# Linear attention: key-value product folded into the output weight, inverse denominators broadcast by DMA, against normalising each attention tile on its own

## The chip, the cores and the metric

The kernel runs on one core of a Trainium2 chip. The metric is device time in microseconds (us) of the whole program; several executions of each kernel are timed, and the median is quoted. The engines have short names in the profile: PE is TensorE (matmuls), PEld its weight loads, DVE is VectorE, ACT is ScalarE, POOL is GpSimd, SP is SyncE, which here only issues DMA transfers. Executions of one kernel agree within about one per cent.

## The reference, cut to what matters

```
def _A_ref(x, wqkv, wo):              # S = 2048 rows, D = 1024, H = 32 heads of 32
    qkv = (x @ wqkv)...               # q, k, v per head
    phi = lambda t: where(t > 0, t + 1, exp(t)) + 1e-6
    pq, pk = phi(q), phi(k)
    kv = einsum("bhsd,bhse->bhde", pk, v)       # 32 x 32 per head
    z = einsum("bhsd->bhd", pk)
    num = einsum("bhqd,bhde->bhqe", pq, kv)
    den = einsum("bhqd,bhd->bhq", pq, z)[..., None] + 1e-6
    return (num / den)... @ wo
x = A_x
h = x + _A_ref(layernorm(x), A_wqkv, A_wo)
h2 = h + _B_ref(layernorm(h), ...)    # a token-mixing MLP: most of the matmul work
```

Because the division is per row and head, `(pq @ kv / den) @ wo` equals `(pq / den) @ (kv @ wo)` when each head's 32 columns of `pq` are scaled first. `kv @ wo` has no row of the sequence in it, so it can be computed once.

## The kernel before

Queries come out transposed: `pqT[p, j, s]` holds feature `j*128+p` (four heads in each group j of 128) of row s. A "q unit" is one group j of 512 rows: eight matmuls, then exp, relu, minimum and a sum. Once the key-value product is complete, each tile i of 128 rows is treated on its own, among the q units of the next 512 rows:

```python
def attn_num_den(i):
    for j in range(ND):                               # ND = 8
        nc.tensor.matmul(nd_ps[:, b, sl*NCOL:(sl+1)*NCOL],   # NCOL = 128 + 4
            lhsT=pqT[:, j, i*P:(i+1)*P], rhs=ndrhs[:, j, :], start=True, stop=True)
    dn = ...; nc.scalar.activation(dn..., ACT.Ln, bias=eps_den[:], scale=1.0)
    rd = ...; nc.scalar.activation(rd[:], dn[:], ACT.Exp, scale=-1.0)     # 1/den
    for b in range(NNB):                              # three PSUM banks
        nc.vector.tensor_tensor(o_sb..., blk[:, :, 0:P]..., rd....to_broadcast(...), ALU.mult)
    return o_sb
def attn_transpose(i, o_sb):
    nc.sync.dma_start_transpose(out=pqT[:, :, i*P:(i+1)*P], in_=o_sb[:])
```

Then the output projection adds the residual. It runs tile by tile:

```python
def out_proj(i):
    xr = xrs.pop(i)                                   # a tile of x, loaded by SyncE
    for dc in range(NDC):                             # two halves of 512 columns
        ap_ = acc_tile()                              # ring of five PSUM banks
        nc.scalar.copy(ap_[:, 0:CW], xr[...])         # seeds the residual
        for j in range(ND):
            nc.tensor.matmul(ap_[:, 0:CW], lhsT=pqT[:, j, i*P:(i+1)*P], rhs=wo_sb[:, j, ...], ...)
        nc.scalar.copy(h_bf[...], ap_[:, 0:CW])
        nc.vector.bn_stats(st[:, dc, :], ap_[:, 0:CW])   # last reader: frees the bank
    ...
    nc.sync.dma_start(h_dram[i][:], h_bf[:])
```

A scheduler puts the instructions of every engine in an order at build time; `pin` keeps an instruction in the order of the program.

## Time and profile before

The median is 573.3 us (572.9 to 573.36, four runs).

| before | us |
|---|---|
| profiled span | 571.5 |
| PE busy | 563.7 (99%) |
| stretch from the first q unit after the key-value product to the mixer's first matmul | 104.4, PE busy in all of it |
| eight num/den matmuls of a tile | 0.47 |
| eight matmuls of 512 columns | 1.73 |

The busy table and the chain that ended last, from the page of the kernel before (share of the span by engine):

```profile
PE 563.7 (99%) x3124; PEld 293.3 (51%) x3124; DVE 390.2 (68%) x759; ACT 272.0 (48%) x585; POOL 1.8 (0%) x8
...
PE 95%; DVE 3%; ACT 1%; issue 1%; DMA 1%; ACTq 0%
```

The same kernel's busy time by windows; columns are the window, its length, and busy us of PE, PEld, DVE, ACT and POOL with counts of instructions, then the granted PE clock and the mean share of the 16 DMA engines and GB/s:

```profile
131.10:235.50 104.40, 104.40 (x577) 51.08 (x576) 81.36 (x196) 72.30 (x173) 0.00 (x0) 1.00 0.59 147
```

TensorE has no idle time there, so only slots on TensorE count. Slots are read as differences of starts, not as durations, since matmuls overlap: below, a group with a duration of 0.63 us holds back the next one by only 0.47. From the timeline of PE (start, duration, what):

```profile
138.47 0.63 PE L1118 MATMUL nd_ps<-ndrhs,pqT 128*128 128x132 bf16 x8
138.94 3.61 PE L1019 MATMUL acc_t<-xnT,wq_sb 128*128 128x512 bf16 x16
142.39 0.63 PE L1118 MATMUL nd_ps<-ndrhs,pqT 128*128 128x132 bf16 x8
...
235.50 1.68 PE L297 MATMUL psA<-hE,wq 128*128 128x512 f16 x7
237.34 0.38 PE L297 MATMUL psA<-hE,wq 128*128 128x512 f16 x1 [0.15 <-DVE hE L1189]
237.55 1.67 PE L297 MATMUL psE<-hE,sa 128*128 128x512 f16 x7
239.96 1.02 PE L297 MATMUL psA<-hO,wq 128*128 128x512 f16 x4 [0.74 <-ACT psB L316]
```

The eight num/den matmuls hold back the next group by 138.94 - 138.47 = 0.47 us; 16 tiles cost 7.5 us. The last rows are the step into the mixer, where PE waited for 0.15 and 0.74 us.

### The profile page before, as it was taken

Reading aid. Unit: us, or ns where it says so; the run is one execution under the profiler, and the core shown is the slowest. Engines: PE = TensorE matmul, PEld = TensorE weight load, DVE = VectorE, ACT = ScalarE, POOL = GpSimd, SP = SyncE. Lnnn points to the kernel's source line nnn. Section 1 sums busy time; section 2 is a strip of 40 time slices with the busy share of each in tenths; the row PEclk is TensorE's granted clock in tenths of the full one; section 3 lists DMA queues with packets and bytes.
Section 4 is the critical chain, followed back from the end, with each engine's and each line's share of the span. In section 5 each row is a group of like instructions: output and inputs, shape, how many; then the busy total and the mean of one; then the engine's idle time right before and its main releaser. Section 6 shows DMA issues by size and latency. Waiting matters only on the chain.

```text
span 571.5 us, 8308 instructions
## 1 busy us (share of the span) xinstructions
PE 563.7 (99%) x3124; PEld 293.3 (51%) x3124; DVE 390.2 (68%) x759; ACT 272.0 (48%) x585; POOL 1.8 (0%) x8
## 2 busy tenths in 40 slices
PE   7999999999999999999999999999999999999997
PEld 3444444455554444346555565555445655645643
DVE  6898887546767879873735627453979749659625
ACT  4747777666667776445445354453220411311211
POOL 1000000000000000000000000000000000000000
PEclk9999999999999999999999999999999999999999
DMA  9933432029536753104041340413892932912111
GB/s 303 357 76 79 89 74 38 19 96 323 118 72 127 177 178 111 55 2 147 1 148 28 120 148 1 148 48 81 205 255 84 244 96 75 278 56 73 38 47 46
DMA packets 97800, 66.61 MB, mean 117 GB/s; under 512 B 32082, under 2 KB 91744, under 8 KB 97760
## 3 DMA queue, kind: packets, MB, share of 16 engines
q1 hardware_dynamic: 97024, 65.42, 41.7%
q10 hardware_dynamic: 672, 0.66, 0.3%
q8 instruction: 24, 0.39, 0.3%
q14 instruction: 16, 0.13, 0.1%
q0 software_dynamic: 64, 0.01, 0.0%
HBM read 50.34 MB, written 8.39 MB: 103 GB/s over the span
## 4 chain that ended last, share of the span: by engine, by line
PE 95%; DVE 3%; ACT 1%; issue 1%; DMA 1%; ACTq 0%
PE psB L297 10%; PE psC L297 10%; PE acc_t L1019 9%; PE acc_t L1167 9%; PE psC L208 7%; PE psA L297 7%; PE psI L230 7%; PE psB L208 6%; PE psI L208 6%; PE psB L750 4%; PE psC L750 4%; PE psA L750 4%; PE psA L208 3%; PE acc_t L674 2%; PE psE L750 2%; PE psE L297 1%
## 5 line engine op out<-in xcount | busy, mean ns | idle before, releaser
L297 PEld LDWEIGHTS <-sa 128*128 128x128 f16 x436 | 42.6, 98 | 46.8 <-issue 0.7
L1019 PE MATMUL acc_t<-xnT,wq_sb 128*128 128x512 bf16 x256 | 58.0, 379 | 0.0
L1167 PE MATMUL acc_t<-wo_sb,pqT 128*128 128x512 bf16 x256 | 56.1, 379 | 0.0
L208 PEld LDWEIGHTS <-wq 128*128 128x128 bf16 (+1 forms) x357 | 34.5, 98 | 31.3
L297 PEld LDWEIGHTS <-wq 128*128 128x128 bf16 (+1 forms) x324 | 31.6, 98 | 33.1 <-issue 1.0
L208 PE MATMUL psC<-gs,wq 128*128 128x512 f16 (+2 forms) x210 | 45.0, 365 | 0.0
L1167 PEld LDWEIGHTS <-pqT 128*128 128x128 bf16 x256 | 24.8, 98 | 29.0
L1019 PEld LDWEIGHTS <-wq_sb 128*128 128x128 bf16 x256 | 24.5, 98 | 27.4
L166 ACT ACTIVATE e_sb<-acc_t 128x512 bf16<-128x512 f32 x40 | 23.9, 597 | 26.5 <-PE acc_t L1019 24.3
L170 DVE TENSOR_SCALAR e_sb<-e_sb 128x512 bf16<-128x512 bf16 x64 | 18.5, 289 | 25.4 <-ACT e_sb L166 24.8
L208 PEld LDWEIGHTS <-sa 128*128 128x128 f16 x231 | 22.6, 98 | 18.6
L750 PEld LDWEIGHTS <-xs 128*128 128x128 f16 x208 | 20.0, 98 | 23.3 <-DVE xs L736 1.3
L208 DVE TENSOR_TENSOR ot<-ot,hr 128x512 bf16<-128x512 bf16 (+2 forms) x27 | 11.2, 415 | 28.1 <-ACT ot L406 27.7
L333 ACT COPY psC<-psB 128x512 f32<-128x512 f32 x22 | 12.5, 570 | 35.1 <-PE psB L297 21.5
L297 PE MATMUL psB<-hT,sa 128*128 128x512 f16 x112 | 28.4, 379 | 0.0
L441 DVE TENSOR_TENSOR e<-psI,es 128x256 f32<-128x256 f32 x12 | 5.1, 425 | 34.0 <-PE psI L230 34.0
L297 PE MATMUL psC<-hT,wq 128*128 128x512 f16 x112 | 28.3, 379 | 0.0
L750 PE MATMUL psA<-wkv,xnT 128*128 128x512 bf16 x104 | 26.7, 379 | 0.0
L1178 DVE BATCH_NORM_STATS2 hst<-acc_t 128x6 f32<-128x512 f32 x32 | 22.1, 692 | 6.7 <-ACT h_bf L1177 6.5
L297 PE MATMUL psA<-hO,wq 128*128 128x512 f16 x112 | 25.6, 379 | 0.7 <-ACT psB L316 0.7
L297 PE MATMUL psB<-hO,sa 128*128 128x512 f16 x112 | 25.5, 379 | 0.0
L297 PE MATMUL psC<-hT,sa 128*128 128x512 f16 x112 | 25.5, 379 | 0.0
(184 smaller groups left out, 1022.9 us busy)
## 6 DMA issues: line engine op xcount, KB each, us to landing
wq<-in_B_w_dram SPq DMA_DIRECT2D x14, 1024.0 KB, 7.7
wq<-in_B_w_dram SPq DMA_DIRECT2D x8, 1792.0 KB, 9.1
xr<-in_A_x_dram SPq DMA_DIRECT2D x16, 256.0 KB, 3.1
h_dram<-h_bf SPq DMA_DIRECT2D x16, 256.0 KB, 2.2
hr<-h_dram SPq DMA_DIRECT2D x32, 128.0 KB, 2.4
out_dram<-ot SPq DMA_DIRECT2D x31, 128.0 KB, 1.8
x_sb<-in_A_x_dram SPq DMA_DIRECT2D x15, 256.0 KB, 3.2
wkv<-in_A_wqkv_dram SPq DMA_DIRECT2D x2, 1024.0 KB, 9.0
```

Source lines behind the costliest of these rows:

```text
L166: pin(nc.scalar.activation(e_sb[:], src, ACT.Exp))
L170: pin(nc.vector.tensor_scalar(e_sb[:], e_sb[:], 1.0, PHI_EPS, ALU.min, ALU.add))
L208: return (lambda *a, **kw: pin(op(*a, **kw))) if Held.on else op
L230: pe.matmul(ps, lhsT=self.lhs[m][:, k, :], rhs=self.mov[m][:, k, :], start=(start and k == 0), stop=(k == self.nk - 1), skip_group_check=True,
L297: pe.matmul(ps[:, cols], lhsT=lhs[:, k, :], rhs=mv(k)[:, cols], start=(start and k == 0), stop=(k == self.nk - 1), skip_group_check=True,)
L333: nc.scalar.copy(self.C[:], self.B[:])
L441: dve.tensor_tensor(self.sts[m].e[:, self.cols(h)], ps, es, ALU.add)
L674: mm = nc.tensor.matmul(pp[:, 0:CW], lhsT=xnT[:, kt, i * P:(i + 1) * P], rhs=wkv[:, kt, c * CW:(c + 1) * CW], start=(kt == 0), stop=(kt == ...
L750: pin(nc.tensor.matmul(ps[:], lhsT=lhs[:, k, :], rhs=rhs[:, k, :], start=(start and k == 0), stop=(k == hk2 - 1), skip_group_check=True,))
L1019: nc.tensor.matmul(qp[:, 0:SW], lhsT=wq_sb[:, kt, j * P:(j + 1) * P], rhs=xnT[:, kt, u * SW:(u + 1) * SW], start=(kt == 0), stop=(kt == ND ...
L1167: nc.tensor.matmul(ap_[:, 0:CW], lhsT=pqT[:, j, i * P:(i + 1) * P], rhs=wo_sb[:, j, dc * CW:(dc + 1) * CW], start=(j == 0 and not SEED_RES ...
L1178: nc.vector.bn_stats(st[:, dc, :], ap_[:, 0:CW])
```

## The change

The intent: replace 128 short matmuls, 48 VectorE evictions and 16 transposing DMAs by one multiplication of wo with the key-value product (8 transposes and 16 matmuls of 512 columns), by 32 matmuls for the denominators, and by scaling the transposed queries in place (8 products on VectorE). The denominators now come out transposed as well (one row per head), so a head's row must be spread over that head's 32 partitions; this is done through DRAM, with a source that repeats. The pieces, with cuts marked by dots:

```diff
-            def attn_transpose(i, o_sb):
-                nc.sync.dma_start_transpose(out=pqT[:, :, i * P:(i + 1) * P], in_=o_sb[:])
...
+            wf = wo_sb[:].bitcast(FP16)           # the folded weight is written over wo
+
+            def fold(j):
+                for c in range(NDC):
+                    cols = slice(c * CW, (c + 1) * CW)
+                    ps = acc_tile()
+                    nc.tensor.matmul(ps[:, 0:CW], lhsT=kvT[:, j, :], rhs=wo_sb[:, j, cols], start=True, stop=True)
+                    if c == 0:
+                        nc.scalar.copy(wf[:, j, cols], ps[:, 0:CW])
+                    else:
+                        nc.vector.tensor_copy(wf[:, j, cols], ps[:, 0:CW])
...
+            def den(u):                           # u: 512 rows
+                ps = ndp.tile([P, SW], F32, tag="den", name="den_ps")
+                for o in range(2):
+                    for g in range(4):            # four column tiles of the array
+                        j = 2 * g + o
+                        nc.tensor.matmul(
+                            ps[g * QR:(g + 1) * QR, :],                   # QR = 32
+                            lhsT=zz[:, j, (1 - o) * HB:(1 - o) * HB + QR],  # HB = 4 heads
+                            rhs=pqT[:, j, u * SW:(u + 1) * SW],
...
+                            tile_position=(0, g * QR),
+                        )
+                rd = a3d.tile([P, SW], FP16, tag="rd", name="rd")
+                nc.scalar.activation(ps[:], ps[:], ACT.Ln, bias=eps_den[:], scale=1.0 / S)
+                nc.scalar.activation(rd[:], ps[:], ACT.Exp, scale=-1.0)
+                pin(nc.sync.dma_start(rd_dram[u][:], rd[:]))
+                for h in range(2):
+                    rdb = a3d.tile([P, NH, SW], FP16, tag="rdb", bufs=3, name="rdb")
+                    for q in range(NH):           # four transfers of 128 KB
+                        j = h * NH + q
+                        r0 = (j // 2) * QR + (j % 2) * HB
+                        pin(nc.sync.dma_start(
+                            rdb[:, q, :],
+                            rd_dram[u][r0:r0 + HB, :].unsqueeze(1).to_broadcast([HB, DH, SW]),
+                        ))
+                    rdbs[u, h] = rdb
+                    if 0 < u < 3:
+                        load_w1(u - 1, h, pin)
+
+            def scale_q(u, h):
+                v = pqT[:, h * NH:(h + 1) * NH, u * SW:(u + 1) * SW]
+                pin(nc.vector.tensor_tensor(v, v, rdbs.pop((u, h))[:], ALU.mult))
...
             for i in range(NS):
-                if i % 2 == 0 and i // 2 < TPC:
-                    attn(NS - TPC + i // 2)
+                if i == 0:
+                    den(NSC - 1)
+                elif i in (1, 3):
+                    scale_q(NSC - 2, i // 2)
+                elif i in (5, 7):
+                    scale_q(NSC - 1, i // 2 - 2)
```

`attn(i)` is the per-tile treatment shown in the section on the kernel before.

The loads of w1 (the mixer's first weights, 1 MB each), which the scheduler could place freely before, are now pinned behind the broadcasts. The edit also pins one sum on VectorE in a later block of the mixer (`nxt.hold = pin`, not shown).

More of the change, by code (lines that the diff above doesn't have):

```diff
@@ L56 @@
     HB = P // DH
-    NCOL = P + HB
-    JPB = BANK // NCOL
-    NNB = (ND + JPB - 1) // JPB
+    QR = P // 4
+    assert ND == 8 and 3 * HB <= QR
     KPB = BANK // (P + 1)
@@ L100 @@
     for q in range(HB):
-        nc.vector.memset(maskbd[q * DH:(q + 1) * DH, q * DH:(q + 1) * DH], 1.0)
+        nc.vector.memset(maskbd[q * DH:(q + 1) * DH, q * DH:(q + 1) * DH], 1.0 / S)
         nc.vector.memset(m4[q * DH:(q + 1) * DH, q:q + 1], 1.0)
@@ L107 @@
     eps_den = const.tile([P, 1], F32)
-    nc.vector.memset(eps_den[:], DEN_EPS)
+    nc.vector.memset(eps_den[:], DEN_EPS / S)
     b1_rows = const.tile([NF, P], BF16)
@@ L134, in w_tile, with load_w1 @@
         return pool.tile([P, n], BF16, tag="wq", name="wq")
-    def load_w1(u, half):
+    def load_w1(u, half, hold=lambda ins: ins):
         if half == 0:
@@ L139, in load_w1 @@
         k = slice(half * NSP, (half + 1) * NSP)
-        nc.sync.dma_start(
+        hold(nc.sync.dma_start(
             w1_tiles[u][:, k, :],
             B_w1[:, u * CW:(u + 1) * CW].rearrange("(k p) f -> p k f", p=P)[:, k, :],
-        )
+        ))
     def load_w2(p, pool):
@@ L218, in __init__, with sums @@
             self.lhs = {1: self.a11, 2: self.a12, 4: self.a22}
-        def sums(self):
+        def sums(self, hold=lambda ins: ins):
             sm = [pools["is"].tile([P, self.nk, P], FP16, tag=self.tag, bufs=pools["is_bufs"], name="is")[:] for _ in range(4)]
-            dve.tensor_tensor(sm[0], self.a21, self.a22, ALU.add)
+            hold(dve.tensor_tensor(sm[0], self.a21, self.a22, ALU.add))
             dve.tensor_tensor(sm[1], sm[0], self.a11, ALU.subtract)
@@ L422, in __init__ @@
             self.mov1, self.mov5 = mov1, mov5
+            self.hold = lambda ins: ins
         def cols(self, h):
@@ L445, in pre @@
                 self.in1 = Inner(self.sts, 1, self.mov1, "i1", self.sink1, self.sum1)
-                self.in1.sums()
+                self.in1.sums(self.hold)
             for st in self.sts:
@@ L585 @@
         a3s = actx.enter_context(tc.tile_pool(name="a3s", bufs=4))
-        a3w = actx.enter_context(tc.tile_pool(name="a3w", bufs=3))
-        a3o = actx.enter_context(tc.tile_pool(name="a3o", bufs=3))
+        a3d = actx.enter_context(tc.tile_pool(name="a3d", bufs=1))
         hstat = actx.enter_context(tc.tile_pool(name="hstat", bufs=1))
@@ L594 @@
         pqT = pqpool.tile([P, ND, S], BF16)
-        ndrhs = pqpool.tile([P, ND, NCOL], BF16)
+        kvbd = pqpool.tile([P, ND, P], BF16)
+        zz = pqpool.tile([P, ND, QR + HB], BF16)
         xctx = ExitStack()
@@ L1084 @@
                 q_fill()
+            nc.vector.memset(zz[:, :, 0:3 * HB], 0.0)
+            nc.vector.memset(zz[:, :, 3 * HB:], float(S))
             for b in range(NKB):
@@ L1087 @@
                 nc.vector.tensor_tensor(
-                    ndrhs[:, j0:j0 + n, 0:P],
+                    kvbd[:, j0:j0 + n, :],
                     kv_ps[b][:, 0:n, 0:P],
@@ L1093 @@
                 nc.vector.tensor_tensor(
-                    ndrhs[:, j0:j0 + n, P:NCOL],
+                    zz[:, j0:j0 + n, HB:2 * HB],
                     kv_ps[b][:, 0:n, P:P + 1].to_broadcast([P, n, HB]),
@@ L1101 @@
         warmctx.close()
+        kvT = xctx.enter_context(tc.tile_pool(name="kvtpool", bufs=1)).tile([P, ND, P], FP16, name="kvT")
         wpool = sactx.enter_context(tc.tile_pool(name="wpool", bufs=2, side="right"))
@@ L1109, with kv_transpose @@
         ndp = a3p.enter_context(tc.tile_pool(name="ndp", bufs=1, space=PSUM))
-        nd_ps = ndp.tile([P, NNB, BANK], F32, name="nd_ps")
-        nc.vector.memset(nd_ps[:], 0.0)
+        rd_dram = [dram.tile([P, SW], FP16, name=f"rd_dram{u}") for u in range(NSC)]
         with ExitStack() as a3:
-            def attn_num_den(i):
+            def kv_transpose():
+                tp = ndp.tile([P, ND, P], BF16, tag="tp", name="kvtp")
                 for j in range(ND):
-                    b, sl = divmod(j, JPB)
-                    nc.tensor.matmul(
-                        nd_ps[:, b, sl * NCOL:(sl + 1) * NCOL],
-                        lhsT=pqT[:, j, i * P:(i + 1) * P],
-                        rhs=ndrhs[:, j, :],
-                        start=True,
-                        stop=True,
-                    )
-                dn = a3s.tile([P, NNB * JPB * HB], F32, name="dn")
-                nc.scalar.activation(
-                    dn[:].rearrange("p (b s c) -> p b s c", b=NNB, c=HB),
-                    nd_ps[:, :, 0:JPB * NCOL].rearrange("p b (s c) -> p b s c", c=NCOL)[:, :, :, P:NCOL],
-                    ACT.Ln,
-                    bias=eps_den[:],
-                    scale=1.0,
-                )
-                rd = a3s.tile([P, NNB * JPB * HB], F32, name="rd")
-                nc.scalar.activation(rd[:], dn[:], ACT.Exp, scale=-1.0)
-                o_sb = a3o.tile([P, D], BF16, name="o_sb")
-                for b in range(NNB):
-                    nsl = min(JPB, ND - b * JPB)
-                    blk = nd_ps[:, b, 0:nsl * NCOL].rearrange("p (s c) -> p s c", c=NCOL)
-                    nc.vector.tensor_tensor(
-                        o_sb[:, b * JPB * P:(b * JPB + nsl) * P].rearrange("p (s h e) -> p s h e", h=HB, e=DH),
-                        blk[:, :, 0:P].rearrange("p s (h e) -> p s h e", e=DH),
-                        rd[:, b * JPB * HB:(b * JPB + nsl) * HB].rearrange("p (s h) -> p s h", h=HB).unsqueeze(3).to_broadcast([P, nsl, HB, DH]),
-                        ALU.mult,
-                    )
-                return o_sb
-            def attn_transpose(i, o_sb):
-                nc.sync.dma_start_transpose(out=pqT[:, :, i * P:(i + 1) * P], in_=o_sb[:])
@@ new lines, in kv_transpose @@
+                    nc.tensor.transpose(tp[:, j, :], kvbd[:, j, :], ident[:])
+                nc.scalar.copy(kvT[:], tp[:])
+            wf = wo_sb[:].bitcast(FP16)
[8 more added lines that the diff above has]
+                        nc.vector.tensor_copy(wf[:, j, cols], ps[:, 0:CW])
@@ new lines @@
+            rds = {}
+            rdbs = {}
+            NH = ND // 2
+            def den(u):
[7 more added lines that the diff above has]
+                            rhs=pqT[:, j, u * SW:(u + 1) * SW],
+                            start=(o == 0),
+                            stop=(o == 1),
+                            skip_group_check=True,
+                            tile_position=(0, g * QR),
[12 more added lines that the diff above has]
+                            rd_dram[u][r0:r0 + HB, :].unsqueeze(1).to_broadcast([HB, DH, SW]),
+                        ))
+                    rdbs[u, h] = rdb
+                    if 0 < u < 3:
+                        load_w1(u - 1, h, pin)
@@ L1169, in out_proj @@
                             lhsT=pqT[:, j, i * P:(i + 1) * P],
-                            rhs=wo_sb[:, j, dc * CW:(dc + 1) * CW],
+                            rhs=wf[:, j, dc * CW:(dc + 1) * CW],
                             start=(j == 0 and not SEED_RESIDUAL),
@@ L1192, in normalize_h @@
                     combine(hE[:, q, :], hO[:, q, :], hT2[:, q, :], hT3[:, q, :], hT4[:, q, :])
-            def attn(i):
-                attn_transpose(i, attn_num_den(i))
             TPC = SW // P
+            for c in range(NDC):
+                load_wo(c)
             for i in range(XRL):
                 load_xr(i)
-            for (u, j) in q_units[8:]:
+            scale_at = {10: (0, 0), 13: (0, 1), 16: (1, 0), 19: (1, 1)}
+            for n, (u, j) in enumerate(q_units[8:]):
                 q_unit(u, j)
-                if u >= 1 and j % 2 == 1:
-                    i = (u - 1) * TPC + j // 2
-                    attn(i)
-                    if i % 2 == 1 and i // 2 < 2:
-                        load_wo(i // 2)
-                    elif i % 2 == 1 and i // 2 < 6:
-                        load_w1(*divmod(i // 2 - 2, 2))
+                if j == 0:
+                    den(u - 1)
+                if n == 1:
+                    kv_transpose()
+                if 4 <= n < 4 + ND:
+                    fold(n - 4)
+                if n in scale_at:
+                    scale_q(*scale_at[n])
             xctx.close()
+            a3w = a3.enter_context(tc.tile_pool(name="a3w", bufs=3))
             hpool = mctx.enter_context(tc.tile_pool(name="hpool", bufs=1, side="right"))
@@ L1266 @@
     cur, nxt = nxt, quad1(1)
+    nxt.hold = pin
     pend = run_pair(cur, pend, nxt, after1=sums1, after5=sums5)
```

## The prediction

The forecast's sum for TensorE came to 0 us, between -1.8 and +4.4. Its term for the denominators was a guess. The terms -7.5 + 0.45 + 3.45 come to -3.6 us. The limits of 0.5 to 1.2 us for a denominator group and the +3 us under "Wrong if" go back to the same guess.

> **What bounds the kernel now.** TensorE. The page's busy table has PE 563.7 of 571.5 us (99%); the chain that ended last is 95% PE; the granted clock is 0.999. In the stretch that the change touches (131.1 to 238 us, busy by windows) PE is busy 106.75 of 106.9 us, DVE 83.8, ACT 73.3. In the waits view PE waits there only for the psB copy (0.7 us) and hE (0.2 us), at the step into the mixer. So only TensorE slots count.
>
> **Slots, from starts in the timeline of PE.** Eight 512-column matmuls take 1.73 us: 216 ns each. Eight 132-column num/den matmuls delay the next group by 0.47 us (138.47 to 138.94): 59 ns each.
>
> **Removed on TensorE:** 16 x 0.47 = 7.5 us.
>
> **Added on TensorE:**
> - kv transposes: eight of 128 columns; eight input transposes (13.60 to 14.04) took 0.44 us: 0.45 us.
> - fold into wo: 16 x 216 ns = 3.45 us.
> - denominators: 4 calls of 8 matmuls, 512 columns, 32 output rows. One after another: 1.73 us a call, 6.9 us in all. They lie in four column groups[...]. This trace has no tiled matmul.[...]
>
> [...]
>
> **Off the chain.** DVE loses 48 scaled evictions (23 us) and a 1.3 us memset, gains 8 in-place products of 128x2048 in 16 bits (1024 columns take 0.66 to 0.69 us, so about 1.3 us each: 10 us) and 8 copies of the fold (about 5 us). ACT loses 8.5 us of narrow Ln/Exp, gains 4 x 1.2 us on 128x512 and about 6 us of copies. The 16 DMA transposes go; 4 MB of broadcast in 1 KB rows come. Each product has many q units (1.73 us each) between request and use, and the ring of three is freed well before the next request. The wo load starts at 123.2 us and landed in 6.4; the fold comes near 140. So I expect no TensorE wait above 1 us on these.
>
> **Small losses:** the first denominators follow the last phi of their rows by one q unit, so PE may wait up to 1 us; the fold makes three PSUM evictions per q unit (ACT 1.8 us of 2.2) and may stall the ring of five by some tenths. The 1 us gap at the step into the mixer (237 to 241) stays, perhaps a little shorter.
>
> **Prediction: 572.7 us, 8 in 10 between 569.5 and 577.** Faster by over 2%: 2%; within 2%: 94%; slower by over 2%: 4%.
>
> **What would show it right:** the time from the first q unit after the kv product (131.1) to the first mixer matmul (235.5) stays 104.4 us within about 2; fold matmuls 216 ns apart; each denominator group 0.5 to 1.2 us from first start to the next full-width start; DVE busy falls by 8 to 12 us with no gain in span; transposing DMA of attention absent.
>
> **Wrong if:** column tiles don't overlap (1.7 us a call: +3 us); the in-order DMA queue holds loads of x or w1 behind broadcasts waiting for the ring, or a product waits for its broadcast and blocks DVE (a PE wait of several us); the scheduler orders the units worse; or the mixer's start moves through w1's loads.

## The result and the profile after

The changed kernel takes 597.0 us in the median (595.75 to 597.95, four runs), 1.041 times the time before (95% interval 1.039 to 1.044). A ratio is the mean time of one kernel's fast runs over that of the other's from the same rounds, so it is not quite the ratio of the medians.

The page of the changed kernel: busy, the rows of PE and of the granted clock in 40 slices of the span (tenths), and the chain:

```profile
PE 570.6 (96%) x3052; PEld 289.9 (49%) x3052; DVE 382.6 (64%) x728; ACT 274.2 (46%) x570; POOL 1.8 (0%) x8
...
PE   8999999999999559989999999999999999999997
...
PEclk9999999999999769989999999999999999999999
...
PE 69%; DVE 12%; DMA 10%; ACT 5%; SPq 2%; issue 2%; ACTq 0%; DVEq 0%
```

Slices 14 to 18, counted from 1, hold the loss. The same stretch as before, first q unit to first mixer matmul, by windows, took 123.72 us for 104.40:

```profile
131.37:255.09 123.72, 109.16 (x505) 47.22 (x504) 72.34 (x158) 75.14 (x158) 0.00 (x0) 0.93 0.44 129
```

The timeline of PE says where:

```profile
133.20 0.62 PE L1144 MATMUL den_ps<-pqT,zz 128*32 128x512 bf16 x8
133.75 1.90 PE L1019 MATMUL acc_t<-xnT,wq_sb 128*128 128x512 bf16 x8
...
141.12 0.59 PE L1129 MATMUL acc_t<-wo_sb,kvT 128*128 128x512 bf16 x2
141.55 1.89 PE L1019 MATMUL acc_t<-xnT,wq_sb 128*128 128x512 bf16 x8
...
181.23 12.69 PE L1191 MATMUL acc_t<-wo_sb,pqT 128*128 128x512 f16 x58
201.18 9.51 PE L1191 MATMUL acc_t<-wo_sb,pqT 128*128 128x512 f16 x32 [7.26 <-ACT acc_t L1189]
217.99 37.27 PE L1191 MATMUL acc_t<-wo_sb,pqT 128*128 128x512 f16 x160 [7.29 <-ACT acc_t L1189]
255.09 1.67 PE L296 MATMUL psE<-hE,sa 128*128 128x512 f16 x7
256.60 2.11 PE L296 MATMUL psA<-hE,wq 128*128 128x512 f16 x9
261.44 0.59 PE L296 MATMUL psE<-hE,sa 128*128 128x512 f16 x1 [2.73 <-DVE hE L155]
```

The tensor work was sized well. A group of eight denominator matmuls starts at 133.20 and the next group at 133.75: 0.55 us, where eight full matmuls of 512 columns take 1.73, so 3.1 times as fast. A pair of the fold takes 141.55 - 141.12 = 0.43 us. But in the output projection TensorE waited twice, 7.26 and 7.29 us, and 2.73 us at the step into the mixer (before: 0.15 and 0.74). After each of the two long waits the same matmuls were slower: the 32 after the first have a duration of 9.51 us, while 32 took 7.07 elsewhere, and the 160 after the second 37.27 where 160 took 34.69 before. The windows just after the waits show the granted clock:

```profile
201.10:205.10 4.00, 3.92 (x10) 1.44 (x10) 2.84 (x8) 2.83 (x10) 0.00 (x0) 0.50 0.17 61
217.90:222.00 4.10, 4.01 (x10) 1.43 (x10) 2.82 (x8) 2.92 (x9) 0.00 (x0) 0.50 0.48 165
```

So 0.50 was granted for about 4 us after each wait; the windows after these show 0.91 (205.1 to 210.7) and 0.85 (222 to 226). How long a wait must be to lower the clock is not shown. After the 2.73 us at the step the granted clock was 0.53 (261.4 to 264.4), and four matmuls that begin 1.2 us later, `psA<-hO,wq`, took 1.78 us. The same four took 1.77 us after a wait of 3.05 us in a run told below (k8), but 1.02 us after 3.05 us (w1early) and 1.03 after 3.01 us (xh_pool). In one run (late) 60 matmuls took 14.81 us after a wait of 2.48 us, where 58 without a wait took 12.69, but 32 took 7.12 us after 3.13 us, where 32 take 7.07 elsewhere. So the two waits cost 14.55 us, and 2.44 + 2.58 us more in clock: 19.6 of the 24.7 us by which the profiled spans differ. Nearly all the rest lies after 255 us: from there to the end 341.1 us against 336.0 before.

What were the waits for? Waits of the changed kernel, longest in total; columns are who waited on whom, us in total, times, longest:

```profile
PE acc_t L1191 <- ACT acc_t L1189: 14.6, 2, 7.3
...
DVE pqT L1172 <- DMA rdb<-rd_dram: 13.1, 3, 8.6
...
ACT acc_t L1189 <- DMA xr<-in_A_x_dram: 10.9, 1, 10.9
ACT h_bf L1201 <- DMA h_dram<-h_bf: 10.5, 1, 10.5
```

VectorE and ScalarE stood waiting for transfers, and TensorE for ScalarE. L1172 is `scale_q`, L1189 the seeding of an accumulator from x, L1201 the copy to h, whose buffer must first have been stored. The timeline of DVE shows the product that waited longest, and what stood behind it in order: a `bn_stats`, which frees an accumulator.

```profile
187.95 0.53 DVE L1213 TENSOR_SCALAR hE<-h_bf,mv_all,sc_all 128x1024 f16<-128x1024 bf16 x1
197.10 1.23 DVE L1172 TENSOR_TENSOR pqT<-pqT,rdb 128x2048 bf16<-128x2048 bf16 x1 [8.62 <-DMA rdb<-rd_dram]
198.24 0.69 DVE L1202 BATCH_NORM_STATS2 hst<-acc_t 128x6 f32<-128x512 f32 x1
```

The timeline of ScalarE shows its two long waits:

```profile
200.54 0.59 ACT L1189 CAST acc_t<-xr 128x512 f32<-128x512 bf16 x1 [10.89 <-DMA xr<-in_A_x_dram]
216.86 0.59 ACT L1201 CAST h_bf<-acc_t 128x512 bf16<-128x512 f32 x1 [10.48 <-DMA h_dram<-h_bf]
```

These ended last: TensorE went on at 201.18 and 217.99, just after ScalarE, while VectorE had its broadcasts at 197.10 and 209.85. So in the change itself the x load and the store of h set the end of both waits; the products went ahead 3.4 and 7.0 us before ScalarE did.

And the DMA view over 138 to 148 us, when nothing but broadcasts of the first denominators was in flight (busy share of 16 engines in tenths, and GB/s, in 40 slices of 0.25 us):

```profile
DMA  0002222222221222222222222222222222222222
GB/s 0 0 0 57 98 94 98 98 82 78 86 70 37 45 94 94 86 94 98 98 94 94 98 94 98 98 94 94 98 94 90 98 82 98 90 90 94 86 98 86
```

Mostly 0.2 at 80 to 98 GB/s, with two short dips: about four of sixteen engines, for 10 us and more per 512 rows. The DMA records of the trace say it more directly: each broadcast gives 5 completion updates where each x load gives 16, and four or five of their packets are in flight 88% of the time (138.5 to 151 us). The first eight broadcasts (1 MB) had landed 14.65 us after the first was issued (137.36 to 152.01). Before the change the two 1 MB loads of wo landed in 5.3 and 7.6 us.

### The profile page after: what moved, and what is told of

Its sections match the earlier page's. It is cut to its first block, busy times and chain, and to the rows that moved or that the text cites. A ratio compares the mean times of both kernels' runs of the same rounds, so it can differ in the third digit from the quotient of the medians.

```text
span 596.2 us, 8140 instructions
## 1 busy us (share of the span) xinstructions
PE 570.6 (96%) x3052; PEld 289.9 (49%) x3052; DVE 382.6 (64%) x728; ACT 274.2 (46%) x570; POOL 1.8 (0%) x8
## 4 chain that ended last, share of the span: by engine, by line
PE 69%; DVE 12%; DMA 10%; ACT 5%; SPq 2%; issue 2%; ACTq 0%; DVEq 0%
PE acc_t L1019 8%; PE psC L207 7%; PE psB L296 6%; PE psC L296 6%; PE psB L207 6%; PE psI L207 5%; PE psA L296 5%; DMA wq<-in_B_w_dram 4%; PE psB L750 4%; PE psC L750 4%; PE psA L750 4%; PE psI L229 3%; PE psA L207 3%; DMA wkv<-in_A_wqkv_dram 2%; DVE sa L288 2%; DVE hst L1202 2%
## 5 line engine op out<-in xcount | busy, mean ns | idle before, releaser
L1191 PE MATMUL acc_t<-wo_sb,pqT 128*128 128x512 f16 x256 | 60.9, 403 | 14.6 <-ACT acc_t L1189 14.6
L1191 PEld LDWEIGHTS <-pqT 128*128 128x128 bf16 x256 | 26.1, 102 | 48.9 <-issue 22.3
L1189 ACT CAST acc_t<-xr 128x512 f32<-128x512 bf16 x32 | 18.8, 589 | 24.3 <-DVE hst L1202 13.2
```

What stands on the lines that cost most here:

```text
L1189: nc.scalar.copy(ap_[:, 0:CW], xr[:, dc * CW:(dc + 1) * CW])
L1191: nc.tensor.matmul(ap_[:, 0:CW], lhsT=pqT[:, j, i * P:(i + 1) * P], rhs=wf[:, j, dc * CW:(dc + 1) * CW], start=(j == 0 and not SEED_RESIDUAL),
```

## The experiments

All timings are medians against runs of the kernel before on the same chip (573.1 to 573.3 us). Theory A: a broadcast whose source starts with 4 rows runs on only 4 DMA engines. That was the guess; it fits the share of 0.2 and the 5 completion updates above, and other numbers of rows were to test it. Rivals: B, the new place of w1's loads; C, the in-order queue of SyncE by its semaphore waits. Later come D, that more source rows are friendlier in some other way than by the number of engines, and E, that VectorE, stuck at the products, is what stops TensorE.

| kernel | median us | ratio, 95% interval |
|---|---|---|
| the change | 597.0 | 1.041, 1.039 to 1.044 |
| spread (16 source rows) | 575.0 | 1.002, 1.000 to 1.004 |
| k8 (8 source rows) | 580.2 | 1.013, 1.008 to 1.017 |
| w1early | 585.1 | 1.020, 1.018 to 1.022 |
| poolq | 576.1 | 1.004, 1.003 to 1.006 |
| actq | 600.8 | 1.047, 1.044 to 1.050 |
| xh_pool | 597.3 | 1.041, 1.040 to 1.043 |
| late | 590.6 | 1.031, 1.029 to 1.032 |
| late_xh | 583.5 | 1.019, 1.017 to 1.020 |
| nobcast (wrong result) | 582.6 | 1.016, 1.013 to 1.018 |
| spread_entry | 573.2 | 0.999, 0.996 to 1.001 |
| spread_w1early_entry | 574.0 | 1.000, 0.998 to 1.003 |

One more, poolq_entry, is told at the end: 575.0, ratio 1.003 (1.001 to 1.004).

### 1. spread: sixteen source rows

The denominators' matmuls have 32 output rows per column tile and used 8 of them. They can hold each head four times at no cost to TensorE (a group takes 133.84 to 134.38, 0.54 us, in spread), and the broadcast then reads 16 rows with 8 copies each.

```diff
+    RH, CP = QR // 2, QR // 2 // HB                       # 16 rows, 4 copies
-            lhsT=zz[:, j, (1 - o) * HB:(1 - o) * HB + QR],
+            lhsT=zz[:, j, (1 - o) * RH:(1 - o) * RH + QR],  # zz holds each head's z in 4 columns
-            r0 = (j // 2) * QR + (j % 2) * HB
+            r0 = j * RH
-            rd_dram[u][r0:r0 + HB, :].unsqueeze(1).to_broadcast([HB, DH, SW]),
+            rd_dram[u][r0:r0 + RH, :].unsqueeze(1).to_broadcast([RH, DH // CP, SW]),
```

The built programs have the same order of instructions on TensorE, ScalarE and SyncE. On VectorE they differ in the shapes of the set-up instructions that write zz, and, by the kept traces, in the place of one sum of h at the step into the mixer (in spread it stands five instructions later, behind the last tile's statistics and not ahead of them). That touches the step into the mixer alone, not the output projection in which the two long waits lay.

> The changed kernel with each head's denominator row produced four times by the column-tiled matmul, so that each broadcast reads 16 source rows with 8 copies each instead of 4 rows with 32 copies. Same bytes, same number of transfers, same instruction order on every engine. Theory A (each broadcast runs on 4 of the 16 DMA engines, which then carry about 90 GB/s and hold up the loads and stores queued behind them): the plateau of DMA share 0.2 at 90 GB/s goes, both waits of TensorE of about 7 us in the output projection shrink below 2 us, the clock is back near 1.0, time 572 to 578 us. Theory B (w1's loads, put behind the broadcasts, are what delays x and h): the waits stay, 590 to 597 us. Theory C (the in-order issuing queue waits on semaphores, whatever the engines do): 588 to 597 us.

Measured: 575.0 us; 22 of the 23.7 us are back. By the profiled spans 19.3 us of the gain lie before the mixer's first matmul (235.83 for 255.09) and 3.2 after it (337.9 us to the end for 341.1), where VectorE's order differs. The whole output projection but for its first six matmuls is one row without a wait in the timeline of PE:

```profile
181.86 54.13 PE L1191 MATMUL acc_t<-wo_sb,pqT 128*128 128x512 f16 x250
```

The DMA view of this kernel over 136 to 146 us (first the store of the denominators, then the same eight broadcasts):

```profile
DMA  0000590000000276286865936847557576000000
GB/s 0 0 0 0 193 316 17 0 0 0 0 0 0 45 246 213 66 270 225 283 193 152 320 82 172 279 131 262 172 184 266 152 250 209 25 0 0 0 0 0
```

The broadcasts now take about 5 us instead of more than 10, and SyncE's issuing of the eight takes as long, 5.10 us (138.00 to 143.10). VectorE waits for no broadcast any more. Each broadcast now gives 16 completion updates, and the first eight landed in 7.0 us instead of 14.65. Theory A holds; B and C fall as sole causes, since w1's loads and SyncE's order are untouched.

### 2. k8: a second dose

The same edit with two rows per head: 8 source rows, 16 copies each.

> A second dose of the same edit as spread: each head's denominator row produced twice, so each broadcast reads 8 source rows with 16 copies each. Order on TensorE, ScalarE and SyncE unchanged. Theory A (number of DMA engines per broadcast set by the 4 source rows, 90 GB/s on 4): plateau of a broadcast alone near share 0.45 and 180 GB/s; time between spread (575) and the change (597), nearer spread: 574 to 582 us, TensorE's two waits below 3 us together. Rival D (16 rows merely happen to be friendlier in another way, for instance in HBM, and the plateau isn't engine-bound): plateau stays at about 90 to 100 GB/s, 588 to 597 us.

Measured: 580.2 us, with the DMA share where A put it; over 136 to 146 us:

```profile
DMA  0770000000245534555534555555555553200001
GB/s 0 254 266 4 0 0 0 0 0 0 45 168 188 148 111 156 193 184 197 193 135 168 176 180 197 193 193 180 197 184 188 188 184 135 90 25 0 0 0 33
```

Share 0.3 to 0.5 and mostly 150 to 197 GB/s: twice the rate of 4 rows. Both waits of the output projection are gone from the profile; what the kernel loses is at the step into the mixer, a wait of 3.05 us followed by a lowered clock (0.92 in the mean of 240 to 262 us). Each broadcast gives 9 completion updates (one more than its rows, as in the change), eight or nine packets are in flight 68% of the time, and the first eight landed in 8.3 us. D falls: 4, 8 and 16 rows give a graded rate and a graded count. This run is the cleaner test, as its trace has the change's order of operations on VectorE, ScalarE and TensorE's weight loads, the step into the mixer included: the stretch from the first q unit to the mixer takes 103.8 us (123.7 in the change), while the loss from there to the end stays (342.6 us; the change 341.1). (The time was more spread than elsewhere, 578.7 to 583.4.)

### 3. w1early: the loads of w1 where they were

```diff
-                    if 0 < u < 3:
-                        load_w1(u - 1, h, pin)
...
+            for u in range(2):
+                for h in range(2):
+                    load_w1(u, h)                          # just after the loads of wo and x
             scale_at = {10: (0, 0), ...
```

> The changed kernel with the four loads of w1 issued just after those of wo, free to be scheduled early as before the change, instead of pinned behind the broadcasts. Theory A: the broadcasts stay on 4 engines (plateau at 0.2 to 0.25 share stays) but they have these to themselves; about half of the loss goes, 577 to 588 us. Theory B: all of it goes, 571 to 576 us. Theory C: a small gain, 585 to 595 us.

Measured: 585.1 us, half of the loss, as A has it; it lies just inside the range of C too (585 to 595). One of the two waits remains (5.8 us); ScalarE then waits 9.2 us for a store of h. So w1's new place makes the congestion worse, but only as long as the broadcasts are slow (a share of 0.25 to 0.26 and 84 to 88 GB/s here, 150 to 180 us): spread has the same place and no waits.

### 4. poolq: another issuing queue

```diff
-                pin(nc.sync.dma_start(rd_dram[u][:], rd[:]))
+                pin(nc.gpsimd.dma_start(rd_dram[u][:], rd[:]))
...                                                        # the 32 broadcasts likewise
```

> The changed kernel with the store of the inverse denominators and the 32 broadcasts issued from GpSimd's queue instead of SyncE's; order on all compute engines unchanged. Theory C (order in SyncE's queue): x loads and h stores no longer stand behind the broadcasts, time 571 to 577 us though the broadcasts still use 4 engines. Theory A: the plateau stays, [...]part of the loss goes and the products still wait for their broadcasts: 578 to 592 us. Theory B: hardly any gain, 588 to 597 us.

Measured: 576.1 us, below what A expected and within what C expected. It is no proof of C, though, as its DMA view over 156 to 166 us shows:

```profile
DMA  0525465657567679676597844332100000000000
GB/s 1 120 82 166 134 262 136 198 181 168 165 150 230 151 214 295 118 198 118 134 232 181 133 99 115 84 98 82 49 16 1 0 0 0 0 0 0 0 0 0
```

The same 4-row broadcasts reach shares of 0.4 to 0.9. So more than four of the sixteen were at work; how they were chosen was not shown. Its packets differ too: of the 1,153 in this window 896 are under 512 bytes and the rest about 4 KB, where the change moves its broadcasts in packets of 1 KB. Also w1's loads, no longer behind anything in SyncE's queue, were issued from 126 us. So this run removes A, B and C at once and can't separate them. My expectation for A here was wrong as to the engines.

### 5. actq: ScalarE's queue

The same edit with `nc.scalar.dma_start`.

> The changed kernel with the store of the inverse denominators and the 32 broadcasts issued from ScalarE's queue: [...]still 4 source rows. w1's loads, freed of their place behind the broadcasts, go early as in w1early. ScalarE pays the issues (32 of about 0.5 us), so this is compared with w1early (585 us). Theory A with a shared ring (the broadcasts hurt by standing ahead of x loads and h stores in one ring): plateau at 0.2 to 0.25 stays, waits for x loads and h stores go, 572 to 579 us. Theory A without it (the 4 engines themselves are too slow for the products): the products' waits for broadcasts stay and the time stays at 582 to 590 us.

Measured: 600.8 us, outside both expectations. ScalarE itself, in order, now stood at the broadcasts, with 11.4 us at the longest, and TensorE waited for ScalarE in the fold (10.5 us) and the q units (3.0 us):

```profile
ACT e_sb L165 <- DMA rdb<-rd_dram: 22.2, 3, 11.4
```

The DMA share in its stretches with broadcasts was again low (0.10 to 0.23 in the windows from 150 to 200 us). The run shows what it costs here to issue transfers that wait from an engine with work on the chain; it does not separate the theories.

### 6. nobcast: no broadcasts at all (wrong)

```diff
-                pin(nc.sync.dma_start(rd_dram[u][:], rd[:]))
-                    for q in range(NH): ... the broadcasts
+                    pin(nc.gpsimd.memset(rdb[:], 1.0))
```

> Wrong result on purpose: the store of the inverse denominators and all broadcasts are taken away; GpSimd fills the buffers with 1.0. Everything else, the fold, the denominators, the products and the pinned w1 loads, stays. All theories: the cost of the tensor work alone, 571 to 574 us (TensorE's sum is 1.4 us below that of the kernel before). If it stays above 577 us, part of the loss comes from the fold or from the scheduler's order at the step into the mixer, not from the broadcasts.

Measured: 582.6 us (two runs), about ten above what all theories expected. The two waits of the output projection are indeed gone. TensorE's waits are elsewhere:

```profile
PE psE L296 <- DVE hE L155: 2.8, 1, 2.8
PE tp L917 <- DVE xn L653: 2.7, 1, 2.7
```

One is at the very start (2.7 us, the first normalised tile late), one at the step into the mixer (2.8 us); after both the matmuls ran slower for a while: the next eight full ones took 3.35 us (1.90 before the change), and four at the step 1.91 us (1.03 in xh_pool). The kept trace has the same sequence of operations as the change on VectorE, ScalarE and TensorE's weight loads, so this kernel is close to the change minus its broadcasts. The stretch from the first q unit to the mixer takes 103.8 us (134.6 to 238.45), as in k8 and spread. The rest of the loss is elsewhere: the first q unit comes 3.2 us later than in the change, and from the mixer's first matmul to the end it takes 341.7 us (the change 341.1, before 336.0). So some 20 us of the change's loss come with the broadcasts, and the 5 us at the step into the mixer and after it stay without them.

### 7. xh_pool: x loads and h stores out of the way

```diff
-                nc.sync.dma_start(xr[:], x[i * P:(i + 1) * P, :])
+                (nc.sync if i < XRL else nc.gpsimd).dma_start(xr[:], x[i * P:(i + 1) * P, :])
-                nc.sync.dma_start(h_dram[i][:], h_bf[:])
+                nc.gpsimd.dma_start(h_dram[i][:], h_bf[:])
```

> The changed kernel with the x loads from the fourth on and the h stores issued from GpSimd's queue; the broadcasts stay in SyncE's queue on 4 engines with w1's loads pinned between them; order on TensorE, VectorE and ScalarE unchanged. Theory A with a shared queue (TensorE waits because x loads and h stores stand behind slow broadcasts in one queue): ScalarE's two waits of 10 us for an x load and an h store go, the first two TensorE waits fall below 3 us together, 574 to 583 us. Rival E (TensorE waits because VectorE, in order, is stuck on the products that wait for broadcasts, 8.6 and 3.7 us): VectorE's waits stay, the accumulators aren't freed, TensorE still waits 5 us or more, 584 to 597 us.

Measured: 597.3 us, no gain at all: rival E. Its waits between 125 and 262 us:

```profile
ACT acc_t L1189 <- DVE hst L1202: 33.3, 22, 10.7
...
DVE pqT L1172 <- DMA rdb<-rd_dram: 19.3, 3, 10.0
...
PE acc_t L1191 <- ACT acc_t L1189: 13.4, 2, 8.3
```

ScalarE now waits for no transfer, only for VectorE's statistics; VectorE waits 19.3 us for broadcasts (13.1 in the change), and TensorE waits 13.4 us as before. So in the change the waits for x loads and h stores ran beside the products' waits, and where they are removed alone, the products' waits stop TensorE for about as long.

### 8. late and late_xh: products later, without and with the above

```diff
-                elif i in (1, 3):
-                    scale_q(NSC - 2, i // 2)
-                elif i in (5, 7):
-                    scale_q(NSC - 1, i // 2 - 2)
+                elif i in (5, 7):
+                    scale_q(NSC - 2, i // 2 - 2)
+                elif i in (9, 11):
+                    scale_q(NSC - 1, i // 2 - 4)
```

> The changed kernel with the last four products placed four tiles later in VectorE's order (tiles 5, 7, 9 and 11 of the output projection instead of 1, 3, 5 and 7). Broadcasts as in the change. If both paths hurt (products blocking VectorE, and x loads and h stores behind the broadcasts in one queue), the second remains: VectorE's waits for broadcasts fall below 3 us, ScalarE still waits 8 us or more for an x load or an h store, 584 to 598 us. If only the products' block matters: 574 to 581 us.

> Both: the last four products four tiles later, and x loads and h stores issued from GpSimd's queue. The broadcasts stay at 4 engines and about 90 GB/s. If these two paths are all by which the slow broadcasts reach TensorE: TensorE's waits in the output projection fall below 2 us in sum and the time to 574 to 580 us, though no broadcast became faster. If a third path exists: TensorE still waits over 4 us there.

Measured: late 590.6 us. VectorE no longer waits for broadcasts, but the other path remains (10.3 us of PE waiting for ScalarE), and TensorE waited 2.5 us for a product directly. Waits of late in the same stretch:

```profile
PE acc_t L1191 <- ACT acc_t L1189: 10.3, 4, 6.5
ACT acc_t L1189 <- DMA xr<-in_A_x_dram: 10.2, 1, 10.2
ACT h_bf L1201 <- DMA h_dram<-h_bf: 5.7, 1, 5.7
```

So either path alone is enough to stop TensorE. Measured for late_xh: 583.5 us, better than either edit alone, but above the 574 to 580 that were expected:

```profile
DVE pqT L1172 <- DMA rdb<-rd_dram: 7.4, 1, 7.4
PE acc_t L1191 <- ACT acc_t L1189: 5.0, 1, 5.0
```

One product still came 7.4 us before its broadcast, four tiles later or not, and TensorE waited 5.0 us for it. With both paths relieved, the broadcasts are simply too late at four engines (a share of 0.23 and 76 GB/s over 137 to 150 us).

### 9. The step into the mixer: spread_entry, spread_w1early_entry, poolq_entry

In the change the scheduler put TensorE's first mixer products in another order: the last part of the fifth product, which needs the last tile's differences, comes early. The edit pins the program's order on TensorE there.

```diff
+        pe.now = not pend                                # pins TensorE's instructions only
         st.p1()
         ...
             st.p5(list(range(st.nk - 1)))
             st.p2(list(range(h)))
             st.p5([st.nk - 1])
+            pe.now = False
```

> The spread kernel with the first products of the first mixer block pinned in program order on TensorE (first product, then seven eighths of the fifth, half of the second, the rest of the fifth), to see how much of what spread still loses lies in the order at the step into the mixer. If it does: the wait for hE of 1.1 us falls below 0.5 and the time to 572.5 to 574 us. If the order there is not it: 574.5 to 576 us as spread.

> Spread, w1's loads early and the pinned order at the step into the mixer, all three: the candidate to beat both kernels. TensorE's sum is 1.4 us below that of the kernel before, so 571 to 574 us.

> The poolq kernel with the pinned order at the step into the mixer: the other candidate to beat both kernels. It should lose the 2 us wait for hE: 572 to 574.5 us. Below 571.5 would mean that the 1.4 us of tensor work saved arrive in the total at last.

Measured: spread_entry 573.2 us, 1.9 below spread, and its ratio to the kernel before is 0.999 (0.996 to 1.001): the same. VectorE's order at the step changed with this edit too, so the 1.9 us are not shown to be TensorE's order alone. Its timeline of PE at the step shows no wait:

```profile
234.89 1.67 PE L296 MATMUL psE<-hE,sa 128*128 128x512 f16 x7
236.40 1.89 PE L207 MATMUL psA<-hE,wq 128*128 128x512 f16 x8
238.13 1.67 PE L207 MATMUL psE<-hE,sa 128*128 128x512 f16 x7
```

With w1's loads early as well: 574.0, no gain. poolq_entry: 575.0, about 1 us below poolq's 576.1, above the range expected; it still waited 1.2 us in the mixer for ScalarE. Neither beats the kernel before. In spread_entry the stretch from the first q unit to the mixer takes 103.8 us (131.1 to 234.89) for 104.4 before; 0.4 of the 0.6 us saved are lost again in the mixer (336.4 us for 336.0), in part to short waits for ScalarE of some tenths each. Why these differ was not followed up.

## Why the prediction was wrong

- *What bounds the kernel; slots.* Right: 216 ns per full matmul held (54.13 us for 250 in spread), and spread_entry, with the whole new tensor work and no wait of TensorE from the q units to the mixer, is equal to the kernel before.
- *The sum of TensorE.* The denominator group was guessed too long; a group took 0.55 us. The fold took 0.43 us a pair as computed. With 0.55 the sum is -7.5 + 0.45 + 3.45 + 2.2 = -1.4 us, within the range -1.8 to +4.4. The stretch in spread_entry shows -0.6; in the last group one of its eight matmuls was placed apart, and its two pieces took 0.73 us (178.47 to 179.20) and 0.32 us (180.60 to 180.92), 1.05 where a whole group takes 0.55.
- *"Each product has many q units ... between request and use, and the ring of three is freed well before the next request ... I expect no TensorE wait above 1 us on these."* This step failed. I counted the time between request and use, and never worked out how long a broadcast takes from its own shape. The only transfer time in that passage is that of the loads of wo (1 MB, 6.4 us in the median). The broadcasts ran on about four engines at about 90 GB/s; 1 MB of them per 512 rows is then some 12 us of moving data, 14.65 us from first issue to last landing even when alone, and longer beside two loads of w1 and the x loads. The products were in VectorE's order before their data came, the queue held x loads and h stores (the x load that ScalarE awaited for 10.89 us was issued at 189.88, after broadcasts whose issue took from 179.46 to 188.39 and a load of w1; the store of h awaited for 10.48 us at 208.13, after eight broadcasts issued from 201.50), and either stopped TensorE, as late and xh_pool show: two waits of 7.3 us where none above 1 us was expected.
- *The clock.* The prediction had no term for it. Two waits of over 7 us cost 5.0 us more at a granted clock of 0.50.
- *The step into the mixer.* "Stays, perhaps a little shorter" was wrong: the new order of TensorE's products there cost 1.9 us in spread (against spread_entry); in the change itself PE waited 2.73 us there, and from the mixer's first matmul to the end it took 4.7 us longer than spread_entry.
- *"Wrong if".* The second item, the in-order queue and a product blocking DVE, is what happened, with one difference: the item has the queue held by broadcasts that wait for the ring, and what held it was their slow flight. It got far too little weight. The first, column tiles that don't overlap, did not.
- *DVE busy falls by 8 to 12 us with no gain in span.* It fell by 7.6 us (390.2 to 382.6), just below what was said.

## What to carry to other kernels

Before trusting a prefetch distance, find out each new transfer's time from its own access pattern, not from its bytes alone: here the same 1 MB, as eight broadcasts, landed in 14.65 us from 4 source rows, in 8.3 from 8 and in 7.0 from 16. If a broadcast has few source rows, a matmul with spare output rows may give it more; here 16 rows took some 20 us of waits and lowered clock out of the output projection. On an engine that takes its operations in order, as VectorE did here with a `bn_stats` behind a product that waited 8.62 us, an operation that needs a transfer should stand as late as its consumer permits (late: 590.6 us for 597.0), and a saving off the critical path is no margin when the operation that waits is ahead of the one that frees the next buffer.
